# One attention and feed-forward kernel, its commands in another order

## The chip, the cores and the metric

The kernel runs on one core of a Trainium2 chip. Five engines work side by side, each through its own queue in order: TensorE (matmuls, PE in the profile), VectorE (DVE), ScalarE (ACT), GpSimd (POOL) and SyncE (SP), which here only starts transfers. The metric is the device time of one execution in microseconds, the median of several runs.

## What is computed

Causal attention over 4 batches of 8 heads, 768 tokens, head size 64, in two kinds: retrieval heads see all earlier keys, the other heads only the first 4 keys and a window of 64. The result, laid side by side for the 8 heads, goes through a feed-forward layer that takes the maximum of three products.

```python
scores = scale * np.matmul(q, k.transpose(0, 1, 3, 2))
stream_keep = causal & (is_sink | in_win)
mask = np.where(retr[0, :, 0, 0, None, None], full_mask, stream_mask)
a = np.exp(scores - max); a = a / (np.sum(a, axis=-1, keepdims=True) + 1e-09)
x = np.matmul(a, v)            # heads side by side: 3072 x 512
h = np.maximum(np.maximum(x @ w1, x @ w2), x @ w3)
return h @ w_out
```

## The kernel before

The work is cut by batch (0 to 3) and by half of the tokens (384 each). The order of everything is written out by hand: `PROGRAM` is a list of 486 short commands, and a loop at the end of `fast` calls one function for each. An engine sees its own instructions in the order of the list, and nothing reorders them; so a command that waits holds up all that stands behind it on that engine. The trailing letters name the engine of a command that several could do: `d` VectorE, `a` ScalarE, `p` GpSimd, `r` a copy done by VectorE as a reduction; for loads, `s` is SP's queue and `c` or `a` ScalarE's.

Batch 0 comes in by half and pair of heads: `hl` loads (`load_first`, L206), `cast` (L220) makes 16-bit copies, `turnp` (`turn_pair`) transposes them on TensorE and evicts with two letters (L241), `s0` (`first_scores`, L608) multiplies and takes the exponential on ScalarE (L629), `k0` multiplies with masks (L377). `vc` and `vt` cast and sort the rows of v (L497, L505, L510). Two more loads of this kind stand in front of the list. Later batches: `load` (L257) brings q and k by GpSimd's queue, casting on the way; `turn` (L272) is a stream transpose on VectorE, eight for a batch; `s` (L674 and L691) and `k` (L377) are scores with exp and masks, eight units a batch. `load_v` (L302) brings v by SP's queue, `v` (`prep_v`, L478) casts it into `va`, and `y` (`prep_x`, L524 and L526) makes the shifted copies `vx` that windowed heads need; `kx`, `kx0` make the far keys alike.

`av` (L717) multiplies with v, and VectorE divides by the sums (L722, L724); with `D` the result is transposed by a DMA on SP's queue (L730), without it by `x` (`turn_x`, L740 and L743) on TensorE. Then the feed-forward: `f b half wi ni` (`hidden`) does four matmuls for one weight (0, 1, 2) and one of six slices. The engine letter evicts weight 0's product (L445); for the two others VectorE takes the maximum (L449). `o` (`output`) does six matmuls, one eviction (L471) and a store. `hidden`, `output`, `av` and the transposes share four PSUM banks, scores have two pairs of banks of their own.

Transfers of weights (`w`) are issued by GpSimd; `gs` is a tiny DMA on SP that waits until a weight has landed, and so holds up SP's queue, and `gp` a tiny copy on GpSimd that waits for a landed pair. `flags` compares the head kinds with those that the list was written for, on GpSimd; `guess` reads the result into a register on every engine; `check`, `verdict` and `read` do the same with the sums, and `general` runs if anything differs. `idle` issues matmuls on zeros. `clear` and `cleark` fill constant parts of `va`, `vx` and `kx`. Buffers rotate: three for loads by `load`, three for `load_v`.

Of the kernel before, what the change touches and what calls it, by code (L numbers as in the profile page):

```python
# [1041 lines left out]
```

## Time and profile before

| | us |
|---|---|
| runs shown: median (lowest, highest) | 190.7 (189.93, 192.7) |
| the profiled execution's span; the page gives no time for it beside the span | 195.2 |
| TensorE busy | 180.9 |
| VectorE busy | 145.0 |
| ScalarE busy | 98.8 |
| GpSimd busy | 81.8 |

Busy is the time in which an engine has an instruction under way; neighbouring instructions overlap by a little. A group's row gives the line, the engine, the operation with its tiles and shapes, the count, the busy time with the mean of one in ns, and then the idle time in front of the group's instructions and what ended it.

### The profile page before, as it was taken

How to read it: one execution, taken by the hardware profiler on the slowest of the kernel's cores; microseconds unless marked ns; L12 is line 12 of the kernel's file. 1: busy time of each engine (PE TensorE's matmuls, PEld its weight loads, DVE VectorE, ACT ScalarE, POOL GpSimd, SP SyncE). 2: the span in 40 equal slices, each digit the busy share in tenths (PEclk: the TensorE clock that was granted, in tenths of full speed). 3: DMA queues.
4: the chain of work that ended last, by engine and by line, in shares of the span. 5: the costliest groups of instructions: out<-in, count | busy, mean ns of one | idle time of the engine just before them, and what ended most of it. 6: DMA issues, size and time to landing. Idle time of an engine off the chain costs nothing.

```text
span 195.2 us, 4739 instructions
## 1 busy us (share of the span) xinstructions
PE 180.9 (93%) x1854; PEld 106.1 (54%) x1854; DVE 145.0 (74%) x308; ACT 98.8 (51%) x158; POOL 81.8 (42%) x140
## 2 busy tenths in 40 slices
PE   7896899998994899999999999999999999999990
PEld 2443646664562445675556565755665566565550
DVE  3758999987997393879897989857794689465541
ACT  3598797377944534679529532775434400211110
POOL 7595978819682296039705600332612500000000
PEclk9999999999999589999999999999999999999999
DMA  5999999999999647935969310241033012401413
GB/s 177 329 325 267 207 213 207 116 164 189 160 187 227 97 133 158 242 99 108 210 167 241 93 58 0 77 114 57 0 66 129 0 57 59 134 0 54 161 54 116
DMA packets 44248, 26.59 MB, mean 136 GB/s; under 512 B 31038, under 2 KB 39742, under 8 KB 44222
## 3 DMA queue, kind: packets, MB, share of 16 engines
q1 hardware_dynamic: 38798, 17.54, 36.8%
q0 software_dynamic: 4192, 7.87, 23.8%
q10 hardware_dynamic: 1232, 0.85, 1.4%
q8 instruction: 15, 0.25, 0.5%
q14 instruction: 11, 0.09, 0.1%
HBM read 25.17 MB, written 6.29 MB: 161 GB/s over the span
## 4 chain that ended last, share of the span: by engine, by line
PE 66%; DMA 12%; DVE 11%; SPq 5%; issue 2%; ACT 1%; ACTq 0%; DVEq 0%
PE yy L437 34%; PE yy L462 15%; DMA vs<-in_v_dram 8%; PE oacc L717 6%; PE st L674 5%; DMA qs<-in_q_dram 4%; SPq L302 4%; DVE KQ L272 4%; PE yst L437 3%; DVE x L724 2%; DVE acc L449 1%; PE yst L462 1%; DVE KQ L241 1%; SPq L283 1%; DVE vx L800 1%
## 5 line engine op out<-in xcount | busy, mean ns | idle before, releaser
L377 POOL TENSOR_TENSOR pt<-pt,kb 128x512 f16<-128x512 f16 (+5 forms) x53 | 48.3, 931 | 67.4 <-ACT pt L691 55.5
L691 ACT ACTIVATE pt<-st 128x1024 f16<-128x1024 f32 (+2 forms) x51 | 43.5, 908 | 24.6 <-PE st L674 24.2
L437 PE MATMUL yy<-xT,w2t 128*128 128x384 f16 x184 | 36.8, 330 | 0.0
L437 PE MATMUL yy<-xT,w0t 128*128 128x384 f16 x180 | 34.9, 326 | 0.6 <-DMA xT<-x 0.6
L437 PE MATMUL yy<-xT,w1t 128*128 128x384 f16 x176 | 34.4, 326 | 0.1
L462 PE MATMUL yy<-woutt,hT 128*128 128x512 f16 (+1 forms) x138 | 32.8, 384 | 0.0
L449 DVE TENSOR_TENSOR hT<-yy,acc 128x384 f16<-128x384 f32 x46 | 25.2, 555 | 6.8 <-PE yy L437 5.1
L449 DVE TENSOR_TENSOR acc<-yy,acc 128x384 f16<-128x384 f32 x44 | 24.0, 555 | 7.9 <-PE yy L437 4.0
L272 DVE STREAM_TRANSPOSE KQ<-kq 128x384 f32<-128x384 f32 x24 | 25.4, 1134 | 0.4 <-DMA kq<-in_q_dram 0.4
L437 PEld LDWEIGHTS <-w0t 128*128 128x128 f16 x192 | 18.1, 98 | 13.5 <-issue 1.7
L445 ACT CAST acc<-yy 128x384 f16<-128x384 f32 x27 | 12.9, 489 | 23.3 <-PE yy L437 21.2
L437 PEld LDWEIGHTS <-w1t 128*128 128x128 f16 x192 | 17.9, 98 | 12.3 <-issue 1.0
L437 PEld LDWEIGHTS <-w2t 128*128 128x128 f16 x192 | 17.8, 98 | 12.3 <-issue 0.9
L462 PEld LDWEIGHTS <-hT 128*128 128x128 f16 x150 | 14.8, 101 | 16.5 <-issue 2.0
L717 PE MATMUL oacc<-va,pt 128*128 128x65 f16 x392 | 19.1, 195 | 4.4 <-ACT va L478 3.5
L717 PEld LDWEIGHTS <-pt 128*128 128x128 f16 x472 | 17.6, 98 | 8.3 <-issue 4.4
L471 ACT COPY ot<-yy 128x512 f32<-128x512 f32 (+1 forms) x14 | 7.9, 566 | 23.6 <-PE yy L462 20.9
L724 DVE TENSOR_TENSOR x<-oacc,sums 128x384 f16<-128x384 f32 x32 | 17.8, 557 | 1.1
L629 ACT ACTIVATE pt<-st 128x1024 f16<-128x1024 f32 (+5 forms) x22 | 15.5, 760 | 3.1 <-PE st L608 2.9
L674 PE MATMUL st<-KQ 32*128 32x128 f16 (+2 forms) x342 | 15.3, 263 | 0.0
L377 DVE TENSOR_TENSOR pt<-pt,kb 128x256 f16<-128x256 f16 (+4 forms) x31 | 11.7, 383 | 1.8 <-ACT pt L691 1.7
L445 DVE CAST acc<-yy 128x384 f16<-128x384 f32 x18 | 10.0, 557 | 3.8 <-PE yy L437 3.3
(117 smaller groups left out, 187.6 us busy)
## 6 DMA issues: line engine op xcount, KB each, us to landing
out_dram<-ot SPq DMA_DIRECT2D x23, 256.0 KB, 2.2
vs<-in_v_dram SPq DMA_DIRECT2D x18, 256.0 KB, 6.0
ks<-in_k_dram SPq DMA_DIRECT2D x8, 192.0 KB, 5.1
kq<-in_k_dram POOLq DMA_DIRECT2D x3, 384.0 KB, 8.1
kq<-in_q_dram POOLq DMA_DIRECT2D x3, 384.0 KB, 9.2
kq<-in_k_dram POOLq DMA_DIRECT2D x3, 288.0 KB, 7.9
kq<-in_q_dram POOLq DMA_DIRECT2D x3, 288.0 KB, 10.0
qs<-in_q_dram ACTq DMA_DIRECT2D x4, 192.0 KB, 4.8
```

The source lines that it names most:

```text
L272: nc.vector.transpose(out=dst.rearrange("c (p j) -> c j p", j=n)[:, j0:j1], in_=src.rearrange("c (j i) -> c j i", i=R),)
L377: engine.tensor_tensor(out=x, in0=x, in1=of_blocks(kb, pattern, rows), op=ALU.mult)
L437: nc.tensor.matmul(yy[:, 0:HALF], w_t[wi][:, ks, ni * P : (ni + 1) * P], xT[b, half, ks].rearrange("p a t -> p (a t)"), start=(ks == 0), s ...
L445: op(out=acc[b, half, ni], in_=yy[:, 0:HALF])
L449: nc.vector.tensor_tensor(out=acc[b, half, ni] if wi == 1 else hT[b, half, ni], in0=yy[:, 0:HALF], in1=acc[b, half, ni], op=ALU.max,)
L462: nc.tensor.matmul(yo[:, 0:n], hT[b, half, ns][:, tb * P : (tb + 1) * P], woutt[:, ns, c : c + n], start=(ns == 0), stop=(ns == NNB - 1),)
L471: op(out=ot[:, c : c + n], in_=yo[:, 0:n])
L629: nc.scalar.activation(out=pts[0, half, hp, u][:, r0:r1, c0:c1], in_=sts[hp][:, r0:r1, c0:c1], func=AF.Exp, scale=sc,)
L674: nc.tensor.matmul(sts["XY"[g // 2]][:, g % 2, c0 : c0 + n * P], KQ[rows, 0, ki * P : (ki + 1) * P] if kind == "p" else kx[b % 2][quad][ro ...
L691: nc.scalar.activation(out=pts[b, s, xy][:, r0:r1, c0:c1], in_=st[:, r0:r1, c0:c1], func=AF.Exp, scale=sc,)
L717: nc.tensor.matmul(o[:, i, r, 0 : D + 1], at[b, h, kind, ki, qi], vv[:, 0 : D + 1], start=(n == 0), stop=(n == len(todo) - 1), skip_group_ ...
L724: nc.vector.tensor_tensor(out=x, in0=o[:, :, :, 0:D], in1=rc.unsqueeze(3).to_broadcast([P, HB, 2, D]), op=ALU.mult,)
```

## The change

`PROGRAM` is replaced by another list. It has the same 486 commands with the same arguments; their order differs from the first line on, and so do engine letters. No function changes. In the start, the clearing commands and `flags` with `guess` stand earlier, pairs 0 and 2 are cast first, and other letters do casts, evictions, far keys and masks. For later batches score units come in another sequence (unit 7 of batch 1 first), v of batch 1 is loaded second half first, the gates between the loads of v are elsewhere, and all attention of batch 3 stands further from the end. The part of the diff up to the middle of batch 1's feed-forward, and the ends of both lists:

```diff
-    "idle 11, hl 0 2 2 sc, cast 0 1 pd, turnp 0 1 aa, cast 0 0 dd, cast 0 2 dp, load_v 0 0 0 4 s",
-    "load_v 0 0 4 4 s, turnp 0 0 ad, cast 0 3 pa, cleark 0 p, cleark 1 d, kx0 0 1 p, s0 0 1 1",
-    "s0 0 0 0, hl 1 0 2 ss, idle 1, turnp 0 3 da, turnp 0 2 da, s0 0 1 0, kx0 0 3 p, s0 0 0 3",
-    "vc 0 0 4 p, vc 0 4 4 p, s0 0 0 1, kx0 0 2 p, s0 0 0 2, hl 1 2 2 ss, cast 1 0 dd",
-    "turnp 1 0 dd, cast 1 3 dd, load 1 0, vt 0 02 da, cast 1 2 aa, vt 0 1 a, cast 1 1 pp",
-    "turnp 1 1 d, w 0, y 0 0 1:4:2 r p, s0 0 1 2, s0 0 1 3, y 0 0 4:5:1 r r, turnp 1 3 ad",
-    "s0 1 3 0, y 0 0 5:8:2 s r, clear 0 d, kx0 1 1 p, y 0 0 1:4:2 s p, s0 1 1 1, load_v 0 1 s",
-    "turnp 1 2 dd, kx0 1 2 r, av 0 0 1, s0 1 2 0, y 0 0 5:8:2 r r, kx0 1 3 r, w 1, gs 1, s0 1 0 1",
-    "av 0 0 0, av 0 0 3, s0 1 0 2, x 0 0 1 d, x 0 0 0 d, load 1 1, s0 1 3 2, vc 1 0 4 p",
-    "x 0 0 3 a, y 0 0 4:5:1 s p, av 0 0 2, vc 1 4 4 p, s0 1 0 0, s0 1 0 3, vt 1 1 a, turn 1 0 0 0",
-    "clear 1 p, k0 1 1 2 p, x 0 0 2 d, vt 1 02 ad, turn 1 0 1 1, turn 1 0 0 1, s0 1 1 0",
-    "k0 0 0 2 p, k0 0 1 2 d, f 0 0 0 3 a, k0 1 0 2 p, f 0 0 0 1 a, s0 1 1 3, w 2, y 0 1 1:4:2 r p",
-    "s0 1 1 2, y 0 1 4:5:1 r r, gs 0, k0 0 3 2 d, f 0 0 0 5 a, kx 1 0 a, k0 2 1 0 p, turn 1 0 1 0",
-    "k0 3 0 2 p, av 0 1 0 D, av 0 1 1 D, f 0 0 0 4 a, turn 1 1 0 0, turn 1 1 0 1, f 0 0 0 2 a",
-    "f 0 0 0 0 a, f 0 0 1 0, load 2 0, f 0 0 1 5, turn 1 1 1 1, s0 1 2 2, k0 2 0 1 p",
-    "turn 1 1 1 0, f 0 0 1 3, f 0 0 1 2, k0 2 0 0 p, y 0 1 5:8:2 r a, f 0 0 1 1, k0 3 1 2 p",
-    "f 0 0 1 4, s 1 0, av 0 1 2 D, kx 1 1 p, k0 2 1 1 p, k0 2 3 1 p, av 0 1 3, f 0 0 2 0",
-    "f 0 0 2 1, s 1 1, f 0 0 2 5, k 1 0 X 1 d, k 1 1 Y 0 p, f 0 0 2 2, turn 2 0 0 0, f 0 0 2 4",
-    "turn 2 0 1 0, x 0 1 3 a, s 1 2, f 0 0 2 3, f 0 1 0 5 a, f 0 1 0 3 a, k 1 1 X 1 p",
-    "turn 2 0 1 1, f 0 1 0 1 d, s 1 7, k 1 2 X 0 p, f 0 1 0 2 d, flags, load_v 1 0 s, v 1 0 0 d",
-    "y 1 0 1:8:2 s a, v 1 0 1 a, gs 0, k 1 2 Y 0 d, y 1 0 4:5:1 s r, k 1 0 Y 0 p, f 0 1 0 0 d",
-    "w 3, v 1 0 2 d, f 0 1 1 2, s 1 3, f 0 1 2 2, f 0 1 1 1, load_v 1 1 s, k 1 3 Y 0 p, f 0 1 1 3",
-    "f 0 1 2 3, y 1 0 4:5:1 r a, y 1 0 1:8:2 r a, gs 0, f 0 1 0 4 d, s 1 5, k 1 0 X 0 d",
-    "k 1 1 X 0 p, load_v 2 0 s, y 2 0 1:8:2 s a, f 0 1 1 5, f 0 1 2 5, y 1 1 1:8:2 r r",
-    "k 1 7 X 1 p, y 1 1 4:5:1 r r, f 0 1 1 4, k 1 5 X 1 p, av 1 0 0 D, s 1 6, load 2 1",
-    "av 1 0 1 D, v 1 1 2 d, f 0 1 1 0, v 1 0 3 a, f 0 1 2 0, f 0 1 2 1, k 1 2 X 1 p, av 1 0 2 D",
-    "av 1 0 3 D, s 1 4, k 1 4 X 1 p, k 1 4 Y 0 p, f 0 1 2 4, v 1 1 3 p, o 0 0 0 a, o 0 0 1 a",
-    "k 1 3 X 1 p, o 0 1 1 a, k 1 7 Y 1 d, turn 2 1 0 1, turn 2 1 1 1, k 1 4 X 0 p, v 1 1 1 p",
-    "turn 2 1 0 0, turn 2 0 0 1, v 1 1 0 p, load_v 3 0 s, v 2 0 0 a, o 0 0 2 a, guess",
-    "turn 2 1 1 0, f 1 0 0 1 a, f 1 0 0 0 a, f 1 0 1 0, f 1 0 0 5 d, k 1 7 X 0 p, v 2 0 1 p",
-    "f 1 0 0 4 d, s 2 0, k 1 3 X 0 p, f 1 0 2 0, k 1 7 Y 0 d, load 3 0, k 1 6 X 0 p, f 1 0 1 4",
-    "k 1 5 Y 0 d, v 2 0 2 a, kx 2 0 d, kx 2 1 a, f 1 0 2 4, f 1 0 1 1, k 1 5 X 0 d, f 1 0 0 3 a",
-    "f 1 0 1 5, f 1 0 1 3, k 1 6 Y 0 p, av 1 1 3 D, av 1 1 1 D, s 2 1, k 2 1 Y 0 p, av 1 1 0 D",
...
-    "f 3 1 1 0, f 3 1 2 0, o 3 0 1 d, o 3 0 2 d, o 3 0 0 a, f 3 1 2 2, f 3 1 2 3, f 3 1 1 1",
-    "f 3 1 2 1, f 3 1 2 4, f 3 1 2 5, o 3 1 0 a, o 3 1 1 a, o 3 1 2 d, idle 1",
+    "hl 0 2 2 sc, clear 0 p, idle 1, idle 11, cleark 1 d, idle 1, cast 0 0 ad, cast 0 2 aa",
+    "flags, turnp 0 0 da, turnp 0 2 ad, s0 0 1 0, s0 0 0 0, clear 1 d, cast 0 3 pp",
+    "load_v 0 0 0 4 s, kx0 0 2 d, cast 0 1 dd, turnp 0 1 aa, kx0 0 1 d, s0 0 1 2",
+    "load_v 0 0 4 4 s, hl 1 0 2 ss, cleark 0 d, s0 0 0 2, turnp 0 3 da, kx0 0 3 r, guess",
+    "vc 0 0 4 p, s0 0 1 1, vc 0 4 4 p, cast 1 0 pp, vt 0 02 dd, y 0 0 1:4:2 s d, hl 1 2 2 ss",
+    "vt 0 1 a, cast 1 2 dd, cast 1 1 pp, turnp 1 1 a, load 1 0, s0 0 1 3, y 0 0 4:5:1 s p",
+    "y 0 0 5:8:2 r p, w 0, y 0 0 5:8:2 s r, s0 0 0 1, cast 1 3 ad, y 0 0 1:4:2 r a",
+    "turnp 1 0 dd, s0 0 0 3, av 0 0 0, kx0 1 1 p, gp 1 2, load 1 1, av 0 0 1, turnp 1 3 ad",
+    "s0 1 3 0, kx0 1 3 d, y 0 0 4:5:1 r r, turnp 1 2 da, kx0 1 2 d, s0 1 2 0, av 0 0 3",
+    "s0 1 2 2, x 0 0 1 a, av 0 0 2, turn 1 0 1 1, w 1, turn 1 0 0 1, s0 1 0 1, s0 1 0 0",
+    "s0 1 1 1, turn 1 0 1 0, x 0 0 0 a, s0 1 1 0, s0 1 1 3, turn 1 0 0 0, k0 0 3 2 p",
+    "x 0 0 2 a, x 0 0 3 a, load_v 0 1 s, vc 1 0 4 p, vc 1 4 4 p, vt 1 02 da, s0 1 0 3",
+    "s0 1 0 2, k0 3 0 2 d, f 0 0 0 1 a, turn 1 1 0 0, s0 1 1 2, k0 2 0 1 d, vt 1 1 a",
+    "y 0 1 5:8:2 r a, s0 1 3 2, k0 2 0 0 d, f 0 0 0 3 a, turn 1 1 1 1, turn 1 1 0 1",
+    "f 0 0 0 0 a, kx 1 1 a, k0 0 0 2 p, k0 1 0 2 d, y 0 1 1:4:2 r a, k0 1 1 2 p, k0 3 1 2 p",
+    "k0 0 1 2 d, load 2 0, w 2, turn 1 1 1 0, kx 1 0 d, f 0 0 0 4 d, k0 2 1 0 p, k0 2 1 1 p",
+    "y 0 1 4:5:1 r d, f 0 0 0 5 d, k0 2 3 1 p, av 0 1 1 D, av 0 1 3, s 1 7, k 1 7 Y 0 p",
+    "k 1 7 Y 1 p, gs 0, av 0 1 0 D, k 1 7 X 0 p, f 0 0 1 0, turn 2 0 0 1, turn 2 0 1 1, s 1 6",
+    "f 0 0 1 5, av 0 1 2 D, s 1 0, turn 2 0 1 0, f 0 0 1 4, f 0 0 1 3, f 0 0 0 2 d",
+    "k 1 6 X 0 p, s 1 5, f 0 0 1 2, k 1 7 X 1 p, k 1 5 Y 0 d, x 0 1 3 a, k 1 5 X 0 d",
+    "f 0 0 1 1, load_v 1 1 s, k 1 0 Y 0 p, k 1 5 X 1 d, k 1 0 X 1 p, s 1 1, k 1 1 X 0 p",
+    "k 1 6 Y 0 d, turn 2 0 0 0, k 1 1 Y 0 p, kx 2 0 p, f 0 0 2 4, f 0 0 2 3, y 1 1 1:8:2 r r",
+    "k 1 1 X 1 d, k 1 0 X 0 d, f 0 1 0 1 a, v 1 1 1 d, s 1 3, y 1 1 4:5:1 r a, f 0 0 2 2",
+    "k 1 3 X 1 d, f 0 1 0 5 d, v 1 1 3 a, f 0 1 1 5, k 1 3 X 0 d, k 1 3 Y 0 p, load_v 1 0 s",
+    "y 1 0 1:8:2 s a, f 0 1 0 2 a, y 1 0 4:5:1 s a, v 1 0 0 p, w 3, s 1 2, f 0 1 1 2",
+    "k 1 2 X 1 p, v 1 1 0 a, y 1 0 1:8:2 r p, f 0 1 2 2, v 1 1 2 d, f 0 1 1 1, v 1 0 2 a",
+    "f 0 0 2 0, v 1 0 1 a, f 0 1 2 1, load_v 2 0 s, k 1 2 Y 0 d, y 2 0 1:8:2 r p",
+    "y 1 0 4:5:1 r d, y 2 0 4:5:1 s a, f 0 0 2 1, v 1 0 3 a, k 1 2 X 0 d, y 2 0 1:8:2 s a",
+    "f 0 1 0 0 a, f 0 1 0 3 a, v 2 0 2 d, f 0 1 1 3, f 0 0 2 5, f 0 1 1 0, f 0 1 2 5",
+    "f 0 1 2 0, av 1 0 3 D, y 2 0 4:5:1 r a, v 2 0 3 a, av 1 0 0 D, f 0 1 0 4 a, f 0 1 1 4",
+    "s 1 4, av 1 0 1 D, av 1 0 2 D, load 2 1, turn 2 1 0 1, gs 0, load_v 3 1 s, load_v 3 0 s",
+    "f 0 1 2 4, k 1 4 X 0 d, turn 2 1 0 0, v 2 0 1 p, k 1 4 X 1 p, o 0 0 0 a, o 0 0 2 a",
+    "av 1 1 0 D, turn 2 1 1 0, kx 2 1 a, turn 2 1 1 1, f 0 1 2 3, k 1 4 Y 0 p, av 1 1 1 D",
+    "o 0 0 1 a, av 1 1 3 D, v 2 0 0 d, s 2 0, k 2 0 X 0 p, k 2 0 X 1 p, av 1 1 2 D",
+    "f 1 0 0 1 d, f 1 0 1 1, f 1 0 2 1, s 2 1, f 1 0 0 3 d, k 2 0 Y 0 d, v 3 1 1 d",
+    "k 2 1 Y 0 d, f 1 0 1 3, k 2 1 X 0 d, load_v 2 1 s, f 1 0 0 4 a, y 3 1 1:8:2 r a",
+    "f 1 0 1 4, y 3 1 4:5:1 r d, s 2 2, k 2 2 X 0 d, f 1 0 0 5 a, f 1 0 1 5, v 3 1 0 p",
+    "y 3 0 4:5:1 r a, v 3 1 2 p, f 1 0 2 5, v 3 0 1 a, f 1 0 0 0 a, f 1 0 1 0, k 2 1 X 1 d",
+    "load 3 0, v 3 0 0 a, y 3 0 1:8:2 s p, k 2 2 X 1 p, y 3 0 1:8:2 r r, v 3 0 2 p",
+    "turn 3 0 0 1, s 2 5, k 2 5 X 0 p, f 1 0 0 2 a, f 1 0 1 2, f 1 0 2 2, turn 3 0 1 1",
+    "f 1 0 2 0, turn 3 0 0 0, v 3 1 3 a, gs 0, s 2 4, o 0 1 2 a, k 2 2 Y 0 p, av 2 0 1 D",
+    "o 0 1 0 d, turn 3 0 1 0, s 2 7, o 0 1 1 d, f 1 1 0 2 a, f 1 1 1 2, f 1 1 2 2",
+    "k 2 4 X 0 p, y 2 1 1:8:2 r a, v 2 1 0 r, av 2 0 0 D, k 2 5 Y 0 p, k 2 5 X 1 p",
+    "y 2 1 4:5:1 r a, v 2 1 3 a, k 2 4 X 1 p, k 2 4 Y 0 d, s 2 6, k 2 6 X 0 d, f 1 1 0 1 a",
...
+    "f 3 0 0 4 a, f 3 0 1 4, f 3 0 2 4, f 3 0 0 5 d, f 3 0 2 3, f 3 1 2 0, f 3 0 2 1",
+    "f 3 0 1 5, f 3 0 2 5, o 3 0 1 a, f 3 1 2 5, o 3 1 1 a, o 3 0 2 a, o 3 0 0 a, o 3 1 0 a",
+    "o 3 1 2 a",
```

52 rows, old and new, of the table PROGRAM are left out of this document.

## The prediction

> **What bounds the kernel now.** I read the page first, then one table of stages.
>
> ```profile
> span 195.2 us, 4739 instructions
> ...
> PE 180.9 (93%) x1854; PEld 106.1 (54%) x1854; DVE 145.0 (74%) x308; ACT 98.8 (51%) x158; POOL 81.8 (42%) x140
> ```
>
> The table of windows (each engine's busy us, then granted clock, DMA share, GB/s), cut at the first transposes, the first stream transpose of batch 1, the stall, the end of the first four output tiles, and the last matmul:
>
> ```profile
> 0.00:5.50 5.50, 4.22 (x11) 1.45 (x11) 2.04 (x9) 1.49 (x2) 4.03 (x13) 1.00 0.63 187
> 5.50:24.90 19.40, 15.56 (x198) 9.42 (x198) 15.18 (x38) 15.75 (x28) 14.88 (x32) 1.00 1.11 280
> 24.90:60.20 35.30, 34.13 (x400) 20.30 (x399) 32.54 (x63) 23.52 (x38) 25.30 (x43) 1.00 1.18 180
> 60.20:73.80 13.60, 10.10 (x73) 5.19 (x71) 8.82 (x14) 6.96 (x10) 6.67 (x11) 0.75 0.67 137
> 73.80:190.50 116.70, 116.70 (x1179) 69.70 (x1177) 86.16 (x188) 50.84 (x80) 30.88 (x42) 1.00 0.39 97
> 190.50:195.20 4.70, 0.20 (x1) 0.00 (x0) 0.30 (x1) 0.27 (x1) 0.00 (x0) 1.00 0.34 120
> ```
>
> From 73.8 to 190.5 TensorE never rests. The commands are the same in both orders, so that stretch can only be longer or shorter by what is already done when it begins. The stage to look at is 24.9 to 60.2: there TensorE is busy 97%, VectorE 92% (32.54 of 35.30), and both hold the time. Before it, ScalarE (15.75 of 19.40), VectorE and GpSimd share the start. Behind it lies one hole: the chain of waits and the waits name it.
>
> ```profile
> 51.10 10.15 DMA vs<-in_v_dram
> ...
> 64.17 0.77 PE oacc L717 x11
> ...
> 67.30 6.47 PE yy L462 x24
> ...
> 108.80 2.59 PE yy L462 x12
> ```
>
> ```profile
> ACT vx L526 <- DMA vs<-in_v_dram: 4.5, 1, 4.5
> ...
> PE oacc L717 <- ACT va L478: 3.5, 1, 3.5
> ```
>
> ```profile
> 60.67:64.17 3.50, 0.01 (x1) 0.10 (x1) 1.68 (x4) 2.85 (x4) 0.00 (x0) 0.83 1.12 207
> 64.17:67.30 3.13, 3.12 (x36) 2.08 (x36) 0.75 (x2) 1.27 (x2) 0.17 (x1) 0.50 0.61 76
> ```
>
> ScalarE's queue stands 4.5 us before a copy out of v of batch 2 (`y 2 0 1:8:2 s a`), whose transfer was issued at 51.10. Behind it are an exp and `v 1 0 3 a`, for which `av 1 0 3` waits on TensorE 3.5 us. Then the clock is 0.50 to 67.30 (3.13 us, half of it lost: 1.6), and 24 output matmuls take 6.47 where twelve take 2.59 later, so 24 should take 5.18: 1.3 more. The hole costs 3.5 + 1.6 + 1.3 = 6.4. The span without it is 188.8; the three runs were 189.93, 190.7 and 192.7. So I take it that the runs shown had a third or so of that hole (1.9 at the median), and that the sum must start from 188.8 + 1.9 = 190.7. What lies around the span isn't on the page; this reading sets it at nothing.
>
> The Trainium skill, "TensorE: Matmul & The Clock Gate", Part 1, says that an idle window of about 3.4 us puts TensorE at half clock until it has been busy for another. The trace agrees here: 3.50 us of idling, then 0.50. By that rule a hole shorter than this would cost itself alone, and one just longer 2.9 us besides.
>
> **The change, part by part.** Both programs hold the same 486 commands; only the order and the engine letters differ. I count work ahead of a point by TensorE time: a group of `hidden` 0.65 us (four matmuls), an output tile 1.29 (2.59 for two), a score unit 0.565, an `av` 0.031 a matmul. The landmark is 60 us of TensorE work, in both orders shortly after batch 1's last scores and a handful of batch 1's `hidden` groups. Up to it VectorE's prices are these:
>
> ```profile
> L272 DVE STREAM_TRANSPOSE KQ<-kq 128x384 f32<-128x384 f32 x24 | 25.4, 1134 | 0.4 <-DMA kq<-in_q_dram 0.4
> L449 DVE TENSOR_TENSOR hT<-yy,acc 128x384 f16<-128x384 f32 x46 | 25.2, 555 | 6.8 <-PE yy L437 5.1
> ...
> L724 DVE TENSOR_TENSOR x<-oacc,sums 128x384 f16<-128x384 f32 x32 | 17.8, 557 | 1.1
> ...
> L722 DVE RECIPROCAL sums<-oacc 128x6 f32<-128x6 f32 x32 | 6.0, 188 | 5.2 <-PE oacc L717 5.0
> ...
> L241 DVE COPY KQ<-tr 128x384 f16<-128x384 f16 x8 | 4.3, 566 | 0.8 <-PE tr L238 0.7
> ...
> L377 DVE TENSOR_TENSOR pt<-pt,kb 128x512 f16<-128x512 f16 x10 | 4.1, 419 | 0.0
> ...
> L377 DVE TENSOR_TENSOR pt<-pt,kb 128x256 f16<-128x256 f16 x11 | 3.5, 318 | 0.0
> ...
> L478 DVE CAST va<-vs 128x384 f16<-128x384 f32 x5 | 2.7, 548 | 0.0
> ...
> L220 DVE CAST kn<-ks 128x384 f16<-128x384 f32 x4 | 2.2, 550 | 1.8 <-DMA ks<-in_k_dram 1.8
> ...
> L510 DVE CAST va<-vb 128x512 f16<-128x512 f32 x2 | 1.4, 686 | 0.2 <-PE vb L505 0.2
> ...
> L743 DVE COPY xT<-tr 128x384 f16<-128x384 f16 x3 | 1.0, 361 | 0.0
> ```
>
> *Attention earlier.* Sixteen `av` lie before the landmark instead of twelve: 4 x (0.557 + 0.188) = 2.98. TensorE has three `hidden` groups and one output tile less there; of these VectorE evicted one: -0.55. An output tile costs VectorE nothing where ScalarE copies it, so `av` in place of outputs is what loads it.
>
> *Letters.* Masks on VectorE: 18 for 8, most of them 256 or 512 wide, 4.32 together (at 318 and 419 ns for these). Casts of v: two more, 1.10. One more eviction of sorted v, 0.69. Far keys and the clearing of kx, small copies: 1.24. Taken off it: two casts of the start (-1.10), two evictions after its transposes, one of them double (-1.52), three of `turn_x` (-1.08), reductions for `prep_x` (-0.56). Sum: 2.98 - 0.55 + 4.32 + 1.10 + 0.69 + 1.24 - 1.10 - 1.52 - 1.08 - 0.56 = 5.5. Sixteen stream transposes stand before the landmark in both.
>
> Means overcount, as neighbours overlap: in the stage from 24.9 to 60.2 the means of the commands sum to 38.2 and the clock shows 35.3, a factor of 0.92. So VectorE has **5.1 us** more to do before the same TensorE work. TensorE can run ahead of it by the four PSUM banks only (three groups, 2 us), which hides an unlucky moment and no steady excess. What VectorE could spare in before: of the 11.9 us of TensorE work between the stall and the landmark it needs about 10.5, so **1.5** of the 5.1 fall into slack. GpSimd loses the masks and has time over, which buys nothing.
>
> *The start.* Rows of the timelines (start us, us, engine, line; idle before and its releaser in brackets):
>
> ```profile
> 5.89 1.27 ACT L241 COPY KQ<-tr 128x384 f16<-128x384 f16 x3 [2.50 <-PE tr L238]
> 8.47 0.51 ACT L220 CAST qn<-qs 128x384 f16<-128x384 f32 x1 [1.31 <-DMA qs<-in_q_dram]
> ```
>
> ```profile
> 7.29 0.55 DVE L220 CAST kn<-ks 128x384 f16<-128x384 f32 x1 [0.59 <-DMA ks<-in_k_dram]
> ```
>
> Before casts and turns pairs 0 and 1, which land first, while pair 2 (7.29) is still under way. After has `cast 0 2 aa` on ScalarE ahead of the eviction of pair 0's query half: ScalarE waits to 7.29, casts twice (0.51 each, to 8.3), evicts 0.49, so the first scores of pair 0 begin near 8.8; pair 1, which before evicts in the row at 5.89, is cast by VectorE only behind pair 2's turn. Following VectorE's queue by these durations to the first `turn 1`, I reach it at 24.6 with 15.5 us of work done, where before stands at 24.9 with 16.9: **1.1 us** behind (1.4 x 0.92). The bounds are 0 (the order of the casts evens out by ScalarE's exps) and 2.5.
>
> *Moved loads and flags.* `flags` on GpSimd goes from the middle to the front of its queue, and `guess` with it, a register load on each engine:
>
> ```profile
> L794 DVEq TENSOR_LOAD <-flagged x1: 691/691/691, 68.0 to 68.0; - x1
> ...
> L794 ACTq TENSOR_LOAD <-flagged x1: 892/892/892, 73.9 to 73.9; - x1
> ```
>
> That is 0 to 0.9 us where the start has no slack; I leave it inside the 1.1. `load 1 0` and the first weights move behind more of GpSimd's casts, about 2 us later, and `load 1 1` ahead of the second weights. They are needed as much later, so I cost them at nothing; the cover gone, it would be 1 to 2 us.
>
> On SP the loads of v of batches 1 and 2 lose the gates between them and come in another sequence (second half, first half, next batch):
>
> ```profile
> 45.23 1.19 SPq L283 DMA_DIRECT2D gates<-w0t  x1
> 46.52 3.85 SPq L302 DMA_DIRECT2D vs<-in_v_dram  x3
> 50.41 0.59 SPq L283 DMA_DIRECT2D gates<-w0t  x1
> ```
>
> That gives 1.9 us with what lies between. But they stay queued behind `av 0 1 2 D`, ahead of which VectorE now has 34.2 us of commands by means instead of 32.0; so they start about as much later. Their reader on ScalarE comes 14 to 15 us of TensorE work behind that point in both orders. I take the hole as in the runs shown, bounds -1.9 (gone) and +6.4 - 1.9 = +4.5 (whole).
>
> *New closeness.* `turn 2 1` and `turn 3 0` now follow their `load` at once in the program, and those loads stand on GpSimd behind copies of v that wait for the same transfers.
>
> ```profile
> kq<-in_k_dram POOLq DMA_DIRECT2D x3, 288.0 KB, 7.9
> ```
>
> A key half lands 7.9 us after its issue. GpSimd comes to `load 2 1` when v of batch 2 has landed, in before at about 61.3; VectorE comes to `turn 2 1` after 43.1 us of commands, at 24.6 + 43.1 x 0.92 = 64.3 and what it waited for v, some 5 us behind GpSimd. Two to 3 us of VectorE's waiting would be left, and two output tiles that ScalarE evicts (1.29 each) stand right behind on TensorE and cover it. Value 0, bounds 0 and 4.
>
> **Sum.** 190.7 + 5.1 - 1.5 + 1.1 = **195.4 us**; the profiled span would be the same with a third of the hole and about 200 with a whole one.
>
> **The rivals.** *The excess is not steady* (no real difference): VectorE's early work is done in moments in which it idled (6.8 us before `hT`, 5.2 before reciprocals), and only the start's 1.1 stays, with half of the waiting for v saved: 190.7 + 1.1 - 1 = 190.8. For it: VectorE is 92%, not 100%, busy in the stage. Against: of its idle time most falls after 73.8.
>
> *The hole was the price all along* (faster): if the runs shown had it whole, and the lost gates let v land 1.9 us sooner, TensorE's 3.5 us fall below 2 and the half clock that followed them goes too; if GpSimd's and ScalarE's letters also hide VectorE's excess, the time is 190.7 - 6.4 + 1.1 = 185.4. It decides where v of batch 2 lands within 2 us of ScalarE's need. Against: the span of 195.2 lies above every run shown, which fits runs without the whole hole better.
>
> *A second hole* (slower still): `turn 2 1` or the reader of v stands over 3.5 us, TensorE runs out of banks and its clock drops as it did at 64.17: 195.4 + 6.4 = 201.8.
>
> **How the numbers follow.** Two per cent, about what a measurement of this kernel can tell, is 3.8 us: faster ends at 186.9, slower begins at 194.5. Forecast 0.43, with an own range of 193 to 198 and a quarter of it under 194.5; no real difference 0.30; hole gone 0.13; second hole 0.14. So faster 0.13, within 0.40 (0.30 + 0.10), slower 0.47. The range of 187 to 200.5 leaves out the hole gone and half of the second hole.
>
> **What would show it.** In the changed profile: the stage up to four output tiles ends 4 to 6 us later against the TensorE work done by then; VectorE above 93% in it; the stretch behind it without a TensorE rest again; ScalarE's first scores after 8.8. Wrong, if VectorE rests for TensorE between 30 and 60, or if the end of the span has holes. What upsets the time most is the clock after the reader of v: a row at 0.50 or none.

## The result and the profile after

The changed kernel takes 197.84 us (median of 5 runs, 197.17 to 200.72), the kernel before 192.7 on the same chip in the same hour (189.93 to 196.03). The ratio is **1.0335, interval 1.0262 to 1.0408**: slower by 3.4%, about 6.4 us. The forecast was 195.4 us, with a range of 187.0 to 200.5, and "slower" at 0.47. The ratio leaves out runs in a slower state, and the profiled run was one of those (200.72 us), so its rows show some us more than a usual run has; where that matters, a row of another run with nearly the same order stands beside it.

The page of the changed kernel, to be read beside the one of before (the same code has other line numbers in each run, as the lists differ in length):

```profile
span 198.9 us, 4743 instructions
...
PE 182.4 (92%) x1854; PEld 106.0 (53%) x1854; DVE 147.3 (74%) x315; ACT 101.4 (51%) x166; POOL 76.7 (39%) x125
```

Work has moved from GpSimd (81.8 to 76.7 us) to VectorE and ScalarE (2.3 and 2.6 more). The run took 200.72, so 1.8 us lie around the span. The prediction had set that at nothing.

The table of windows after (busy us of TensorE, its weight loads, VectorE, ScalarE and GpSimd, then clock, DMA share, GB/s):

```profile
5.60:25.00 19.40, 16.32 (x175) 8.82 (x174) 13.77 (x38) 14.51 (x27) 14.09 (x31) 0.91 1.11 279
25.00:58.00 33.00, 29.91 (x366) 17.80 (x366) 30.87 (x61) 28.44 (x49) 18.42 (x24) 1.00 0.95 174
58.00:78.00 20.00, 19.64 (x255) 12.59 (x254) 18.49 (x40) 11.13 (x19) 9.01 (x15) 1.00 1.06 168
78.00:112.00 34.00, 29.91 (x311) 16.57 (x310) 27.31 (x52) 20.47 (x35) 15.38 (x21) 1.00 1.17 169
112.00:152.00 40.00, 40.00 (x501) 25.12 (x500) 30.75 (x75) 17.16 (x23) 15.38 (x16) 1.00 0.21 51
```

Before, TensorE never rested from 73.8 on. The same stretch of before:

```profile
78.00:112.00 34.00, 34.00 (x404) 20.83 (x402) 29.25 (x63) 22.60 (x35) 16.05 (x23) 1.00 0.74 164
```

Now it rests 4.1 of the 34 us between 78 and 112. The DMA engines move hardly more there (169 against 164 GB/s), but by the profile's count they are busier, 1.17 against 0.74. The hole of before near 61 is gone. The timeline names the new rests (start, length, engine, line; idle before and its releaser):

```profile
25.55 0.23 PE L612 MATMUL st<-KQ,kx 64*128 64x128 f16 x2 [0.90 <-ACT pt L633]
30.92 0.21 PE L612 MATMUL st<-KQ,kx 64*128 64x128 f16 x1 [0.99 <-ACT pt L633]
...
82.88 0.81 PE L441 MATMUL yy<-xT,w0t 128*128 128x384 f16 x4 [0.87 <-DVE acc L453]
94.33 0.48 PE L441 MATMUL yy<-xT,w0t 128*128 128x384 f16 x2 [0.56 <-DMA xT<-x]
108.93 0.81 PE L441 MATMUL yy<-xT,w2t 128*128 128x384 f16 x4 [0.72 <-ACT ot L475]
111.25 0.33 PE L678 MATMUL st<-KQ 32*128 32x384 f16 x1 [1.22 <-DVE KQ L276]
```

The early two are waits for ScalarE's exponentials in batch 0. Of the four late ones shown two wait for VectorE, one for a DMA transpose and one for ScalarE's copy of an output tile; only the last, 1.22 us, waits directly for a stream transpose of q or k. VectorE's own timeline shows that it stands there for q and k of batch 3, whose stream transposes follow close behind their `load`.

```profile
87.36 1.13 DVE L276 STREAM_TRANSPOSE KQ<-kq 128x384 f32<-128x384 f32 x1 [1.19 <-DMA kq<-in_k_dram]
90.42 1.13 DVE L276 STREAM_TRANSPOSE KQ<-kq 128x384 f32<-128x384 f32 x1 [0.88 <-DMA kq<-in_q_dram]
...
104.67 1.13 DVE L276 STREAM_TRANSPOSE KQ<-kq 128x384 f32<-128x384 f32 x1 [0.67 <-DMA kq<-in_k_dram]
108.09 1.13 DVE L276 STREAM_TRANSPOSE KQ<-kq 128x384 f32<-128x384 f32 x1 [2.29 <-DMA kq<-in_q_dram]
```

The chain of work that ended last names two long transfers in this stretch (start, us):

```profile
84.64 9.65 DMA xT<-x
...
96.15 11.85 DMA kq<-in_q_dram
```

The first is a DMA transpose of `av`, issued at 84.64, while the q of `load 3 0` was under way (issued at 78.48, landed 11.9 us later). The second is the q of `load 3 1`, and the next DMA transposes were issued beside it. In before the transposes of this stretch took 3.0 us (median of the four issued from 76 to 95), and no load of q or k was under way when they were issued.

So two places: a start that is late, and transfers of batch 3's q and k that run beside DMA transposes. To see how much each holds, I added up TensorE's matmuls in the order of the timeline, each at its bare time (384 columns 0.1625 us, 65 columns 0.031, and so on), and noted when each kernel had done the same amount. A few matmul records are missing, so an entry is good to about a microsecond. The rows below the first two are experiments told further down.

| us of TensorE work done | 15 | 20 | 30 | 45 | 60 | 100 | span |
|---|---|---|---|---|---|---|---|
| before (profiled with the hole, 6.4, between 45 and 60) | 28.0 | 33.2 | 43.1 | 60.2 | 80.9 | 121.1 | 195.2 |
| after (the profiled run of 200.72) | 32.1 | 38.7 | 49.9 | 65.5 | 79.8 | 126.1 | 198.9 |
| `read_later` (order of before, no hole) | 28.9 | 34.1 | 44.1 | 60.2 | 76.4 | 117.1 | 191.1 |
| `start_of_after` | 31.1 | 36.3 | 46.1 | 61.6 | 78.0 | 118.9 | 192.9 |
| `no_vector_masks` | 31.6 | 37.5 | 49.2 | 63.9 | 78.8 | 122.4 | 195.1 |
| `loads_3_alone` | 30.8 | 37.3 | 48.4 | 63.8 | 82.1 | 122.4 | 195.0 |
| `before_masks_to_vector` | 28.2 | 34.0 | 44.8 | 61.8 | 76.5 | 117.9 | 192.0 |

Ahead of 45 the clock fell to about half for some 3 us in `after`, `read_later`, `start_of_after` and `no_vector_masks`, and not in `before`, `loads_3_alone` and `before_masks_to_vector`. The cleanest pair for the start is therefore `before` and `loads_3_alone`: 2.8 us apart at 15, and 3.6 at 45. After and the runs that share its order are 2 to 4 us behind at 15, and 3.5 to 5 behind at 45. From 20 to 45 all kernels take much the same, 25.3 to 27.8 us for 25 us of work. Then from 60 to 100 after loses again: 46.3 us, against 40.2 in before. `no_vector_masks`, whose late order is that of after, takes 43.6 there in a usual run.

### The profile page after: what moved, and what is told of

It reads as the page before. It is cut to its first block, busy times and chain, and to the rows that moved or that the text cites. A ratio compares the mean times of both kernels' runs of the same rounds, so it can differ in the third digit from the quotient of the medians.

```text
span 198.9 us, 4743 instructions
## 1 busy us (share of the span) xinstructions
PE 182.4 (92%) x1854; PEld 106.0 (53%) x1854; DVE 147.3 (74%) x315; ACT 101.4 (51%) x166; POOL 76.7 (39%) x125
## 4 chain that ended last, share of the span: by engine, by line
PE 64%; DMA 13%; ACT 10%; DVE 6%; issue 4%; SPq 1%; POOL 0%; DVEq 0%; ACTq 0%
PE yy L441 34%; PE yy L466 11%; PE oacc L721 6%; DMA kq<-in_q_dram 6%; PE st L678 5%; DMA xT<-x 5%; ACT pt L633 4%; PE yst L441 3%; DMA ks<-in_k_dram 2%; DVE pt L381 1%; ACT pt L695 1%; PE vb L509 1%; PE yst L466 1%; DVE KQ L276 1%; PE st L612 1%
## 5 line engine op out<-in xcount | busy, mean ns | idle before, releaser
L381 POOL TENSOR_TENSOR pt<-pt,kb 128x512 f16<-128x512 f16 (+5 forms) x49 | 44.0, 916 | 48.8 <-ACT pt L695 33.8
L441 PE MATMUL yy<-xT,w0t 128*128 128x384 f16 x184 | 36.7, 326 | 1.4 <-DVE acc L453 0.9
L441 PE MATMUL yy<-xT,w2t 128*128 128x384 f16 x184 | 36.1, 326 | 1.6 <-ACT ot L475 0.7
L466 PE MATMUL yy<-woutt,hT 128*128 128x512 f16 (+1 forms) x138 | 31.4, 372 | 0.2 <-DVE hT L453 0.2
L475 ACT COPY ot<-yy 128x512 f32<-128x512 f32 (+1 forms) x16 | 9.1, 567 | 29.5 <-PE yy L466 29.5
L466 PEld LDWEIGHTS <-hT 128*128 128x128 f16 x150 | 14.2, 98 | 14.9 <-issue 0.2
L381 DVE TENSOR_TENSOR pt<-pt,kb 128x512 f16<-128x512 f16 (+5 forms) x35 | 16.0, 473 | 4.2 <-ACT pt L695 2.6
L678 PE MATMUL st<-KQ 32*128 32x128 f16 (+2 forms) x342 | 16.1, 257 | 1.5 <-DVE KQ L276 1.2
L633 ACT ACTIVATE pt<-st 128x1024 f16<-128x1024 f32 (+5 forms) x22 | 16.1, 776 | 1.5 <-PE st L612 1.2
L678 PEld LDWEIGHTS <-KQ 32*128 32x128 f16 x342 | 9.2, 92 | 8.1 <-issue 7.1
## 6 DMA issues: line engine op xcount, KB each, us to landing
ks<-in_k_dram SPq DMA_DIRECT2D x8, 192.0 KB, 4.5
qs<-in_q_dram ACTq DMA_DIRECT2D x4, 192.0 KB, 4.2
```

The lines of the kernel that those rows point to most:

```text
L381: engine.tensor_tensor(out=x, in0=x, in1=of_blocks(kb, pattern, rows), op=ALU.mult)
L441: nc.tensor.matmul(yy[:, 0:HALF], w_t[wi][:, ks, ni * P : (ni + 1) * P], xT[b, half, ks].rearrange("p a t -> p (a t)"), start=(ks == 0), s ...
L466: nc.tensor.matmul(yo[:, 0:n], hT[b, half, ns][:, tb * P : (tb + 1) * P], woutt[:, ns, c : c + n], start=(ns == 0), stop=(ns == NNB - 1),)
L475: op(out=ot[:, c : c + n], in_=yo[:, 0:n])
L633: nc.scalar.activation(out=pts[0, half, hp, u][:, r0:r1, c0:c1], in_=sts[hp][:, r0:r1, c0:c1], func=AF.Exp, scale=sc,)
L678: nc.tensor.matmul(sts["XY"[g // 2]][:, g % 2, c0 : c0 + n * P], KQ[rows, 0, ki * P : (ki + 1) * P] if kind == "p" else kx[b % 2][quad][ro ...
```

## The experiments

Theory 1: the start, and the late loads of batch 3, cost the time. Theory 2, the prediction's: VectorE's extra early work sets the pace between 30 and 66 us.

**The start of the one with the rest of the other.**

```diff
 start_of_after: commands 1 to 94 of the changed list, through "s0 1 3 2"
-the rest in the changed order
+the rest in the order and with the letters of the kernel before
```

> The first 94 commands of after, then what is left in the order and with the letters of before. The slower start as the cause: 196 to 197, all of it but what later slack absorbs. VectorE's excess as the cause, or the late loads: 192 to 193, since neither is left.

194.32 us (193.65 to 196.77), ratio 1.0186 (1.0122 to 1.0251). The new start with the old rest loses 1.9%, some 3.5 us. In the table it is 2 to 3 us behind at 15 to 30, and 1.4 to 1.8 behind `read_later` from 45 to 100; one rest of TensorE, 1.84 us at 63.79 for VectorE's division, is not in the profile of either kernel and may be the mixture's own (`read_later` has one of 0.62 for a division at 63.01). So the start is worth 1.7 to 3.5 us.

```diff
 start_of_before: commands 1 to 91 of the kernel before, through "s0 1 1 2"
-the rest in its own order
+the rest in the changed order, with the changed letters
```

> The first 91 commands of before (through the scores of batch 0), then all that is left in the order and with the letters of after. If the slower start is what costs (6.8 us behind before at 30 us of TensorE work in the two traces), the time falls from 197.8 to about 192. If VectorE's steady excess costs, the start gives back only its letters and its idling, about 2: 196. If the waits for the late loads of q and k between 78 and 112 us cost, they stay: 196 to 197.

202.19 us (201.18 to 203.33), ratio 1.0649 (1.0503 to 1.0794): slower than both. The seam made a wait of its own, as `flags` and `guess` met there and TensorE stood 3.82 us for the flag. So it was tried once more with both later, alone and with two loads moved:

```diff
 clean_start_of_before: as start_of_before, and
-flags ... guess
+flags, guess, o 0 0 0 a
```

> The first 91 commands of the kernel before (up to its `s0 1 1 2`), then the rest in the changed kernel's order with its letters, and `flags` with `guess` just before the first output tile, so that no engine meets the register load at the seam. Theory 1 (the start costs about 3.5 of the 7 us): 197.5 - 3.5 = 194, and TensorE has done 20 us of work at 33 to 34 us as in the kernel before. Theory 2 (the order behind the start holds VectorE's excess of 5 us, and the start only 1.1): 196.4 or more.

```diff
 start_and_loads: as clean_start_of_before, and
+load 3 0, k 1 4 X 1 p
...
+load 3 1, k 2 2 X 1 p
```

> Both of the two edits: the start of the kernel before with late `flags` and `guess`, and the two loads of batch 3 moved ahead. Theory 1 (start and late loads are all that was lost): 190 to 191, the time of the kernel before without its hole. Theory 2 (an excess of VectorE of 3.6 to 5 us stays): 194 or more. If the two costs overlap, 192.

202.87 us (202.02 to 203.71) and 202.67 (201.92 to 204.01): 6 us or more above every figure that was expected. The timelines of `clean_start_of_before`, of GpSimd and TensorE, show one reason:

```profile
66.92 1.14 POOL L378 TENSOR_TENSOR pt<-pt,kb 128x512 f16<-128x512 f16 x1 [4.31 <-ACT pt L692]
68.02 0.09 POOL L755 MEMSET want<- 1x8 f32 x1
...
70.32 0.17 POOL L767 CAST flagged<-both 1x2 int32<-1x2 f32 x1
```

```profile
71.24 4.44 PE L463 MATMUL yy<-woutt,hT 128*128 128x512 f16 x12 [4.07 <-POOL flagged L767]
```

The small instructions of `flags` stood on GpSimd behind a mask that waited 4.31 us for an exp; every engine waited for the flag, and TensorE's clock was 0.57 for the 4 us behind. It isn't the only one. From 28 to 37 us, long before that flag, TensorE of this run rests 3.1 us of 9, more than half of it for a mask on GpSimd (1.75 us at 34.80), and the clock is 0.54 in the 3 us behind. So the changed rest doesn't follow the old start without waits of its own. These three runs say nothing of the split; the price of the start rests on `start_of_after` and on the table.

**Letters.**

```diff
 letters_of_before: the changed order, each command
-with its changed engine letter
+with the letter that it has in the kernel before
```

> The order of after, every command with the engine letter that it has in before. VectorE's excess as the cause: of the 5.5 us counted, the letters are 3.1 (masks, casts, far keys), the earlier attention 2.4, so about 195. The slower start as the cause: only as far as letters make it, 195 to 198. The late loads as the cause: 197.8 as before the edit.

234.96 us (233.24 to 237.47), ratio 1.2312 (1.2052 to 1.2572). GpSimd's queue now stands 9.2 us for v in one `y`, and its masks come too late for `av` (7.6 us of TensorE's waits). The letters fit the order that they were found with: put back alone, the old ones win nothing. What part single letters have isn't shown by this.

**VectorE's work, taken off and put on.**

```diff
 no_vector_masks: the changed kernel without 16 commands ahead of "o 0 0 1 a"
-k0 3 0 2 d, k0 2 0 1 d, k0 2 0 0 d, k0 1 0 2 d, k0 0 1 2 d
-k 1 5 Y 0 d, k 1 5 X 0 d, k 1 5 X 1 d, k 1 6 Y 0 d, ...
```

> The changed kernel without the 16 masks that VectorE multiplies before the first output tiles (5 `k0` and 11 `k` with the letter `d`); those keys stay unmasked, so the sums and the outputs differ. The masks take 7.0 us of VectorE between 30 and 66 us. Theory 2 (the prediction's: VectorE's early work sets the pace between 30 and 66): the lag of 4 to 5 us behind the kernel before is gone by 45 us of TensorE work, and the time is 192.5 to 194. Theory 1 (the lag is there already at 31 us and comes from the start, VectorE's masks lie beside TensorE work): 196 to 197.5.

196.55 us (195.85 to 197.12), ratio 1.0277 (1.021 to 1.0344). Its windows, to be held against after's:

```profile
25.00:58.00 33.00, 31.16 (x368) 18.42 (x368) 28.05 (x49) 28.39 (x49) 19.34 (x26) 0.95 0.96 179
...
78.00:112.00 34.00, 32.32 (x370) 18.27 (x369) 28.13 (x55) 22.59 (x38) 15.85 (x21) 1.00 1.04 164
```

VectorE loses 2.8 us of busy time in the first of them (30.87 to 28.05). At 45 us of work TensorE stands at 63.9, as `loads_3_alone` with all its masks does at 63.8. The clock hides a part: here it was 0.54 from 25 to 28 us and 0.89 in the next 3, which costs at most 1.7 us, and `loads_3_alone` had no such dip. But the whole run gains only about 1 us, the intervals of the two ratios overlap, and every run lies above the 192.5 to 194 of theory 2. Theory 2 falls for the changed order, as far as the masks go; the earlier `av`, its other part, was not tested alone.

```diff
 before_masks_to_vector: the kernel before with 8 masks
-k0 1 0 2 p, k0 3 0 2 p, k0 2 0 1 p, k0 2 0 0 p, k 1 1 X 1 p, k 1 2 X 0 p, k 1 5 X 1 p, k 1 3 X 1 p
+k0 1 0 2 d, k0 3 0 2 d, k0 2 0 1 d, k0 2 0 0 d, k 1 1 X 1 d, k 1 2 X 0 d, k 1 5 X 1 d, k 1 3 X 1 d
```

> The kernel before with 8 masks that the changed kernel has on VectorE given from GpSimd to VectorE (`k0` 1 0 2, 3 0 2, 2 0 1, 2 0 0 and `k` 1 1 X 1, 1 2 X 0, 1 5 X 1, 1 3 X 1), nothing else. Theory 2: VectorE has 3.3 us more before 60 us, 1.5 of it in slack, so the undisturbed runs go from 190.3 to 192 or 193. Theory 1 (VectorE's masks lie beside TensorE work): 190 to 190.5, and the runs that are longer by the hole stay as they were.

193.82 us (193.08 to 194.75), ratio 1.0144 (1.0093 to 1.0195): 2.7 us slower. In the order of before VectorE's work does have a price. TensorE waits for masks on VectorE, 1.4 us of the 2.7:

```profile
30.69 0.20 PE L719 MATMUL oacc<-va,pt 128*128 128x65 f16 x1 [0.86 <-DVE pt L379]
39.70 0.20 PE L719 MATMUL oacc<-vx,pt 128*128 128x65 f16 x1 [0.57 <-DVE pt L379]
```

So theory 2 names a true price of the one order, and it isn't the price of the other, whose TensorE work is already late by its start. That this lateness is the reason is argued here, not shown.

**ScalarE in the start.** The table of windows from 17 to 34 us, before and then after:

```profile
17.00:34.00 17.00, 14.47 (x194) 9.06 (x193) 16.18 (x37) 14.01 (x25) 14.44 (x21) 1.00 1.12 210
```

```profile
17.00:34.00 17.00, 13.80 (x168) 8.04 (x167) 14.52 (x29) 16.71 (x30) 12.42 (x20) 1.00 1.09 204
```

ScalarE is busy 98% there, 82% before; VectorE has more time. Theory 3 was that ScalarE holds the start:

```diff
 x_by_vector: in the changed list
-x 0 0 1 a, ... turn 1 0 1 1, ... turn 1 0 0 1, ... turn 1 0 1 0, x 0 0 0 a, ... turn 1 0 0 0, ... x 0 0 2 a, x 0 0 3 a
+x 0 0 1 d, ... x 0 0 0 d, ... x 0 0 2 d, x 0 0 3 d, turn 1 0 1 1, turn 1 0 0 1, turn 1 0 1 0, turn 1 0 0 0
```

> The changed kernel with its four early evictions after TensorE transposes (`x 0 0 0` to `x 0 0 3`) given from ScalarE to VectorE, and the four stream transposes of batch 1 that stand among them moved right behind the last of them. Theory 3 (in the start ScalarE holds TensorE: it is 98% busy from 17 to 34 us and the first `hidden` groups wait for its evictions and exps): ScalarE loses 1.9 us there, the second `hidden` group begins near 29.5 in place of 31.0, and the time is 195 to 196. Theory 2 (VectorE's work sets the pace): 1.4 us more on VectorE, 198 to 199. No difference: 197 to 197.6.

200.01 us (198.85 to 200.58), ratio 1.0446 (1.0377 to 1.0516): slower. TensorE now waits where masks stand behind the four transposes:

```profile
36.55 0.20 PE L718 MATMUL oacc<-vx,pt 128*128 128x65 f16 x1 [2.02 <-DVE pt L378]
```

The edit took work off ScalarE and put a block on VectorE that is just as late. ScalarE's full queue is seen in the windows and in the two rests ahead of scores; that it alone causes the late start isn't shown.

**The loads of batch 3.** Three edits tried to take away VectorE's waits for them.

```diff
 loads_earlier: in the changed list
+load 2 1, w 3
+load 3 0, k 1 4 X 1 p
+load 3 1, k 2 2 X 1 p
```

> After, with load 2 1, load 3 0 and load 3 1 moved ahead on GpSimd's queue (before w 3, before k 1 4 X 1 and before k 2 2 X 1), so that no stream transpose follows its own load. The late loads as the cause: the 4 us that TensorE rests between 78 and 112 go, about 194. The start or VectorE's excess as the cause: 197 to 198, the waits turn into waits for VectorE.

```diff
 loads_3_alone: as loads_earlier, without
-load 2 1, w 3
```

> The changed kernel with `load 3 0` moved to just before `k 1 4 X 1 p` and `load 3 1` to just before `k 2 2 X 1 p`, nothing else; `load 2 1` and the weights stay where they were. Theory 1 (the loss behind 78 us is the waiting for q and k of batch 3, three rests of 0.5 to 1.2 us and the banks that run empty around them): 197.5 - 3.5 = 194, and no TensorE rest over 0.3 us between 80 and 112. Theory 2 (VectorE has 5 us more to do and the waits only show where it would be late anyway): 197 to 198, with TensorE resting elsewhere for VectorE in the same stretch.

199.51 us (197.09 to 200.65), ratio 1.0512 (1.0413 to 1.0611), and 197.29 (196.81 to 200.39), ratio 1.0359 (1.0316 to 1.0402). Behind 80 us of either run TensorE has no rest of 0.4 us more: `loads_3_alone` has 34.00 busy of 34 where after has 29.91, and goes from 60 to 100 us of work in 40.3 us, as before does. Yet nothing is won: the loss lies earlier, and from 45 to 60 us of work `loads_3_alone` takes 18.3 us where `no_vector_masks` takes 14.9. In `loads_earlier` the output weights came late (TensorE 1.26 us at 66.6). In `loads_3_alone` VectorE and then TensorE stood here:

```profile
71.73 0.56 DVE L726 TENSOR_TENSOR x<-oacc,sums 128x384 f16<-128x384 f32 x1 [2.96 <-DMA xT<-x]
```

```profile
72.35 0.30 PE L719 MATMUL oacc<-va,pt 128*128 128x65 f16 x4 [1.21 <-DVE x L726]
74.33 0.61 PE L676 MATMUL st<-KQ 32*128 32x384 f16 x15 [0.88 <-DVE KQ L274]
```

The division had no free `x` buffer, as a DMA transpose that reads one was late, and the load now ran beside it. These are the same four transposes (`av 1 1` with `D`) in both kernels, with their median time from issue to landing, first in `loads_3_alone` (62 to 68 us), then in the changed kernel (63 to 69):

```profile
xT<-x SPq DMA_TRANSPOSE x4, 8.1
```

```profile
xT<-x SPq DMA_TRANSPOSE x4, 4.9
```

In `loads_earlier` they took 7.8 us, in `no_vector_masks`, where `load 3 0` comes later, 4.4. The last edit left `load 3 0` where it was, moved its readers back, and moved `load 3 1` ahead:

```diff
 turns_3_later: in the changed list
-load 3 0, ... turn 3 0 0 1, ... turn 3 0 1 1, ... turn 3 0 0 0, ... turn 3 0 1 0
+load 3 0, ... load 3 1, ... turn 3 0 0 1, o 0 1 0 d, ... turn 3 0 1 1, ... turn 3 0 0 0, ... turn 3 0 1 0
```

> The changed kernel with the four commands `turn 3 0` moved some 5 us later on VectorE, behind other work of the same stretch, so that they no longer wait for `load 3 0`, which stays where it is; `load 3 1` moved to just before `k 2 2 X 1 p`, where it caused no rest in the two runs that had it there. Theory 1 (about 3 us of the loss are waits for q and k of batch 3 behind 78 us; to move `load 3 0` ahead only moved the waiting to the DMA transposes): 197.3 - 3 = 194 to 195, no TensorE rest over 0.4 us from 60 to 112. Rival (the order of batch 2 and 3 loses its 3 us in another way): 196.5 to 198.

201.93 us (199.53 to 203.03), ratio 1.0505 (1.0419 to 1.0591). Up to 70 us of work it is ahead, at 89.1 against 91.9 of `loads_3_alone`; then:

```profile
94.76 0.48 PE L438 MATMUL yy<-xT,w0t 128*128 128x384 f16 x1 [3.83 <-DMA xT<-x]
96.04 0.80 PE L438 MATMUL yy<-xT,w0t 128*128 128x384 f16 x2 [0.80 <-DMA xT<-x]
```

```profile
94.00:97.00 3.00, 1.44 (x5) 0.55 (x5) 1.73 (x2) 0.13 (x1) 0.00 (x0) 0.50 1.17 198
97.00:100.00 3.00, 3.00 (x22) 1.70 (x23) 1.12 (x3) 1.53 (x4) 0.00 (x0) 0.50 1.12 227
```

Again the transposes were late, this time with both loads of batch 3 beside them: the four issued from 77 to 85 us took 15.3 us (median), where those from 78 to 85 in the changed kernel, beside `load 3 0` alone, took 11.1. TensorE waited 3.83 us, and half clock came behind. So the waits behind 78 us can be taken away, and each way that I tried turned them into another wait on a transfer. No run keeps all loads of batch 3 clear of the transposes. That this meeting costs about 3 us is what fits; that some order of these commands would win them back isn't shown.

**The hole of the kernel before.**

```diff
 read_later: the kernel before with one command moved
-load_v 2 0 s, y 2 0 1:8:2 s a, f 0 1 1 5
+load_v 2 0 s, f 0 1 1 5
...
-o 0 0 0 a
+y 2 0 1:8:2 s a, o 0 0 0 a
```

> The kernel before with one command moved: `y 2 0 1:8:2 s a`, the copy on ScalarE that waits for v of batch 2, from behind `load_v 2 0 s` to just before `o 0 0 0 a`. If the hole at 60.7 us of the kernel before comes from that copy standing ahead of `v 1 0 3 a` in ScalarE's queue, every run lies at 189 to 191 and no profile shows a rest over 1.5 us near 60 us; the mean of the runs falls by 2 to 3 us against the kernel before. If the hole comes from the transfer itself, whoever waits for it, the times stay spread from 189 to 196.

191.34 us (189.88 to 194.8, 12 runs), against 192.64 for the kernel before beside it (189.65 to 202.91, 18 runs); ratio 1.002 (0.9971 to 1.007). Its one profile has no rest over 0.7 us near 60, which fits the theory that the command moves the hole's wait away. But runs of 192.5 to 194.8 remain, which the first theory excluded: the hole is not the only cause of the spread. It isn't faster than the kernel before by an amount that can be measured.

## Why the prediction was right, and where it wasn't

The direction, the class and the range held: 195.4 was forecast, 1.2% below the 197.84. The steps that led there mostly did not, and their errors partly cancelled; that the number came so near is luck.

- **The starting point** of 190.7 was made of 188.8 and "a third of the hole". Of these the second was wrong: span and time differ by some 1.8 us in the runs above (196.81 with 195.0, 192.88 with 191.1). So 188.8 is 190.6 in time without any hole, and the runs of 193 and more were the ones with something in them. The number stood, for another reason.
- **VectorE's 5.1 us more before the landmark** is there: by 60 us of TensorE work it is busy 67.62 us after and 62.78 before, 4.8 more. But the step "1.5 of the 5.1 fall into slack" failed. `no_vector_masks` takes 7.0 us of masks off VectorE and gains about 1 us, so in this order the masks' work lay nearly all beside other work, where the sum had put 3.6 of the 5.1 on the path. The rule by which I refused that ("hides an unlucky moment and no steady excess") fits the order of before, as `before_masks_to_vector` shows; as I read it, it needs TensorE to be ready otherwise, and here it was not. "Wrong, if VectorE rests for TensorE between 30 and 60" didn't warn either: VectorE was busy 93% of 25 to 58, as forecast, and still didn't set the pace. The share couldn't tell: `read_later`, in the order of before, has VectorE busy 30.90 of the same 33 us.
- **The start** was mis-sized: 1.1 with bounds 0 and 2.5, measured at 1.7 to 3.5, and with the stage right behind it at 3.6 (63.8 against 60.2 at 45 us of work). Its mechanism was at most half of it. ScalarE's casts did wait to 7.00, as foreseen, and the first exp came at 8.69, but before's first exp stands at 8.88. VectorE reaches the four stream transposes of batch 1 at 25.01 (forecast 24.6). Up to that point the forecast holds: counted from the matmuls in the traces, `loads_3_alone` has about 1 us less TensorE work done at 25 us than before, for the 1.4 foreseen. The rest is lost behind it: at 40 us it is 3 to 4 us less. ScalarE has 2.7 us more to do from 17 to 34; that this is the cause isn't shown.
- **New closeness** was valued 0 with bounds 0 and 4. "Two output tiles ... stand right behind on TensorE and cover it" holds for `turn 2 1`: no rest stands there. It failed for `turn 3 0`, and more so for `turn 3 1`, which I hadn't priced at all. Nor had I priced what the loads do to the DMA transposes beside them (11.1 us in place of 3.0). With 3.6 lost by 45 us of work, about 3 of the 6.4 are left for this stretch, and `no_vector_masks` loses about as much from 60 to 100 (43.6 against 40.2 in before). The sentence "the stretch behind it without a TensorE rest again" was plainly wrong.
- **The hole as in the runs**: v landed in time, and no profile of the changed order has it. That is the mechanism of the rival "the hole was the price all along"; its price was not what bound the time.

In sum: 190.7 + 3.6 + about 3 = 197.3, with about 1 us for VectorE's masks somewhere in it, where the prediction had 190.7 + 1.1 + 3.6 + 0. The 3.6 is measured at equal work; the 3 is what is left, and fits the late stretch.

## What to carry to other kernels

Compare two orders at equal TensorE work: it shows at once in which stretch time is lost, and guards against pricing a busy engine that isn't the one waited for. A count of extra work on an engine is a price only where another engine would otherwise have been ready; ask what is late already. In a stretch where loads, stores and DMA transposes share the queues, a transfer moved ahead isn't free: ask which small transfer now runs beside it, and who waits for that one. Read the time from issue to landing by stretches: the median over the whole changed kernel (4.0 us for 27 transposes) hides the 11.1 us of the stretch that loses time.

## What the runs showed of the hardware that was not expected

*A mask on VectorE took longer beside one on GpSimd.* Timelines of VectorE and GpSimd in the changed kernel:

```profile
57.36 1.56 DVE L381 TENSOR_TENSOR pt<-pt,kb 128x1024 f16<-128x1024 f16 x1
```

```profile
57.18 1.18 POOL L381 TENSOR_TENSOR pt<-pt,kb 128x512 f16<-128x512 f16 x1
```

A mask of this shape with no mask on GpSimd beside it took 0.69 us (in `loads_3_alone`, at 29.68). Here it began 0.18 after GpSimd's and ended 0.56 after it (58.92 and 58.36), so it looks as if it had waited and then run. The Trainium skill, "SBUF — State Buffer", section "SBUF: two separate sides", says that a VectorE instruction with two inputs in SBUF and a GpSimd instruction that reads SBUF take a shared port in turn, the later one blocked for the whole of the other. This pair agrees: 58.36 and 0.69 make 59.05, 0.13 us past the measured end. The prediction took all masks at their mean.

*The clock drops without a long rest.* In `no_vector_masks`:

```profile
22.00:25.00 3.00, 1.66 (x29) 1.09 (x30) 2.87 (x8) 2.85 (x5) 1.83 (x3) 1.00 1.16 213
25.00:28.00 3.00, 2.78 (x25) 1.63 (x26) 3.00 (x4) 3.00 (x6) 1.78 (x2) 0.54 1.09 211
```

No rest before 25 is longer than 0.90 us behind 14, and TensorE was busy 55% of the 3 us ahead; still the clock was 0.54 in the next 3. Other runs have the same dip at another time, or none (`loads_3_alone`, 1.00 throughout the start), in both orders. The rule that the prediction took from the Trainium skill, "TensorE: Matmul & The Clock Gate", Part 1, an idle window of about 3.4 us, doesn't cover this: no window of that length was without work here.

*A casting load of q and k and the DMA transposes issued beside it both took longer.* The four transposes of `av 1 1` took 8.1 and 7.8 us from issue to landing with `load 3 0` beside them, 4.9 and 4.4 without. In the changed kernel between 78 and 85 us, with `load 3 0` beside them:

```profile
xT<-x SPq DMA_TRANSPOSE x4, 11.1
```

The key half of that load took 9.4 us and the query half 11.9, where they took 5.9 and 7.4 in before (70 to 95 us). Whether the cast, the shared engines or the bytes do it isn't shown.
